# Moving the w_down stores to SyncE and three of eight outer products to VectorE in the feed-forward stage of a training-step kernel

## The chip, the cores and the metric

The kernel runs on one core of one Trainium2 chip. Its time is the device time of one execution in microseconds. The core has five instruction streams that run beside each other: TensorE (PE: matmuls and transposes), VectorE (DVE), ScalarE (ACT), GpSimd (POOL) and SyncE (SP). In this kernel POOL and SP do nothing but issue DMA transfers, except for a few constants that POOL builds at the start. Each of them takes its transfers strictly in the order of the program: one whose semaphores are not there yet holds up all that stand behind it. Three runs of the kernel before took 605.4, 604.7 and 602.12 us, so the median is 604.7 us.

## The reference

The reference is the forward and the backward pass of one decode step of a transformer block with one token (a row `x` of 1024 numbers). The six modulation vectors are `silu(c) @ w_mod`; then comes attention of 32 heads over the last 4096 rows of a key/value cache of 65536 rows, and then a feed-forward part:

```
g = x @ w_gate;  u = x @ w_up            # 1024 -> 3584
y = (sigmoid(g) * u) @ w_down            # 3584 -> 1024
```

The outputs are the result row and the gradients with respect to the input row, both caches, and all weight matrices. Two facts shape the work. The gradient of the caches is zero outside the 4096 rows, yet all of it must be written: about 126 MB of zeros. And the gradient of each weight matrix is an outer product of two vectors, so that each weight is read once and a matrix of the same size is written: there is little arithmetic for many bytes. For the feed-forward part, the gradients of `w_up` and `w_gate` are outer products of the normalised row `h2` with `dug` (the gradient at `u` and `g`), and that of `w_down` is one of the hidden vector with the gradient of the output.

## The kernel before

All large tiles lie in one on-chip array, `arena`; buffers are places in it, and the order of all instructions is written out by hand (`tc.manual_schedule()`), engine by engine. Dependences become semaphore waits. The 120 zero regions, 1 MB each, are stores that `zero(n)` (line 153) puts into POOL's stream at fixed places, `n` at a time from tables such as `Z_FFN`, as filling between the other transfers.

The stages follow each other: loads and attention (to about 155 us of the profile), a long matmul stage for the gradient of the output projection (`bch`, line 692, to about 285 us), the feed-forward stage (about 310 to 483 us), and a last stage that writes the gradients of the attention weights, of `w_mod` and of the caches (to the end at 605 us). The change touches the feed-forward stage alone.

That stage goes over seven blocks `q` of 512 hidden units. A block holds 2 MB of `w_up` and `w_gate` in `ug_v`, which has two buffers (`q % 2`), each in eight pieces `j` of 128 rows; and 1 MB of `w_down` in `wd_v`, which has one buffer in two halves `s` of 0.5 MB. Every buffer is used in place: the weights are loaded, read, overwritten with their own gradient, stored, and the weights of a later block are loaded over them.

In one pass of the loop (line 1017) these steps follow each other:

1. For each `j`: `ttr` (line 210, DVE) multiplies the piece of block `q` with the broadcast row `dug_b`, writes the product over the piece and sums it into `dh2acc`; then `outer_act` (line 241, ACT) overwrites the piece with `h2[j] * dug_b`. At `j` 0, 2, 5 and 6 a `side()` job is put in ahead of the outer product: eight PE transposes of another tensor into the one `mm` bank of PSUM (line 837), and an ACT copy of the result (line 838).
2. `store_ug` (line 869, POOL) stores pieces 0 to 3 after `j == 3` and pieces 4 to 7 after the loop, two transfers of 0.5 MB each time.
3. `front(q+1)` (line 954, PE) multiplies the next block's weights with `h2`, `gates` (lines 959 and 960, ACT) takes two sigmoids, `hh_ops` (line 193, DVE) forms the hidden vector.
4. For each half `s` of `w_down`: `ffn_mm` (line 971, PE), `wd_ttr` (two `ttr` on DVE, writing `junk`) and `wd_outer` (two `outer_dve`, line 206, DVE), and then `store_wd` (line 855), which POOL issues.
5. `dug_part` (lines 193, 990 and 991; DVE, PE, ACT) makes the next `dug_b`.
6. Loads for later blocks: `load_ug(q+2, 0, 4)` and `load_ug(q+2, 4, 4)` (line 865, POOL) into the buffers that block `q` leaves, and `load_wd(q+2, 0)`, `load_wd(q+2, 1)` (line 852, SP).

Three orders matter. In POOL's stream of one block stand, in this order: `load_ug` of pieces 0 to 3, `store_wd` of half 0, `store_wd` of half 1, `load_ug` of pieces 4 to 7, two zero regions, `store_ug` of pieces 0 to 3, one zero region, `store_ug` of pieces 4 to 7. A `load_ug` waits until the `store_ug` of the same pieces has landed. In SP's stream stand the `load_wd` alone, each of which waits until the `store_wd` of its half has landed. Transfers of POOL share eight completion semaphores in turn, and so do those of SP and ACT together.

In the last block there is no `side()`; instead ACT copies six parked tiles back from PSUM (`unpark`, line 1000), three of them within the loop over `j`, at 3, 5 and 6.

Of the kernel before, what the change touches and what calls it, by code (L numbers as in the profile page):

```python
# [58 lines left out]
def kernel(  # L59
# [26 lines left out]
    nc = tc.nc  # L86
# [13 lines left out]
    def ar(off, size):  # L100
        return arena[:, int(off * KIB):int((off + size) * KIB)]

    def vt(shape, name, dt=FP32):
        return pool.tile(shape, dt, name=name)
# [47 lines left out]
    def zero(n, after=None):  # L153
        for _ in range(n):
            if len(zleft) <= keep[0]:
                return
            region, narrow_ = zleft.pop(0)
            first = None
            if narrow_:
                nc.gpsimd.inc_swdge_sem([], [], mode="reset_dge_cursor")  # L160
                n = nlen - ncount.pop()
                first = nc.gpsimd.dma_start(
                    out=rest[0:NS, 0:nlen * 128].rearrange("p (t x) -> p t x", t=2)[:, :, n * 64:(n + 1) * 64],
                    in_=zeros[0:NS, 0:64].rearrange("p (t x) -> p t x", t=1).broadcast_to([NS, 2, 64]))
                ins = nc.gpsimd.dma_start(
                    out=region[8:P, :].bitcast(FP32).rearrange("(t p) x -> p t x", t=2),
                    in_=zeros[0:60, :].rearrange("p (t x) -> p t x", t=1).broadcast_to([60, 2, ZW // 2]))
            else:
                ins = nc.gpsimd.dma_start(out=region.bitcast(FP32), in_=zeros[:, :])  # L169
            if after is not None:  # L170
                dep(first or ins, after)
# [26 lines left out]
    def addv(out, a, b):  # L198
        return tt(out, a, b, ALU.add)

    def cp(out, a):
        return nc.vector.tensor_copy(out=out, in_=a)  # L202
# [6 lines left out]
    def ttr(out, w, b, acc):  # L209
        return nc.vector.tensor_tensor_reduce(out=out, in0=w, in1=b, scale=1.0, scalar=0.0,  # L210
                                              op0=ALU.mult, op1=ALU.add, accum_out=acc)
# [28 lines left out]
    def outer_act(out, col, b):  # L240
        return nc.scalar.activation(out=out, in_=b, func=ACT.Copy, scale=col)  # L241
# [203 lines left out]
    def side(n=1):  # L445
        for _ in range(n):
            if jobs:
                jobs.pop(0)()
# [177 lines left out]
    for g in range(G):  # L626
        nbank = bank_pair("n_ps", g)
        for t_ in range(KT):
            s = g * KT + t_
# [216 lines left out]
    wd_v = ar(152, 8).rearrange("p (i d) -> p i d", i=4)  # L846

    def wd_dram(t, q, s):
        return t[q * FB + s * 256:q * FB + s * 256 + 256, :].rearrange("(p j) d -> p j d", j=2)

    def load_wd(q, s):
        nc.sync.dma_start(out=wd_v[:, 2 * s:2 * s + 2, :], in_=wd_dram(B_w_down, q, s))

    def store_wd(q, s):
        nc.gpsimd.dma_start(out=wd_dram(out_8, q, s), in_=wd_v[:, 2 * s:2 * s + 2, :])

    def ug_part(view, q, j0, n):
        return view[:, j0:j0 + n, q * FB:(q + 1) * FB]
# [4 lines left out]
    def load_ug(q, j0, n):  # L863
        for k, view in ((0, wu_view), (1, wg_view)):
            nc.gpsimd.dma_start(out=ug_tile(q, k, j0, n), in_=ug_part(view, q, j0, n))

    def store_ug(q, j0, n):
        for k, view in ((0, dwu_view), (1, dwg_view)):
            nc.gpsimd.dma_start(out=ug_part(view, q, j0, n), in_=ug_tile(q, k, j0, n))  # L869
# [17 lines left out]
    h2 = vt([P, KD], "h2")  # L887
# [49 lines left out]
    dug_b = scr  # L937
# [10 lines left out]
    def front(q):  # L948
        gu = gu_t[q % 2]
        for col, k in ((4, 0), (0, 1)):  # L950
            for i in range(4):
                f0 = 256 * (i // 2) + i % 2
                for j in range(KD):
                    nc.tensor.matmul(gu[:, col + i:col + i + 1], lhsT=ug_v[:, q % 2, j // 4, j % 4, k, f0:f0 + 255:2],
                                     rhs=h2_bf[:, j:j + 1], start=(j == 0), stop=(j == KD - 1))

    def gates(q):
        r, gu = small[q % 2], gu_t[q % 2]
        nc.scalar.activation(out=r["sg"], in_=gu[:, 0:4], func=ACT.Sigmoid)
        nc.scalar.activation(out=r["om"], in_=gu[:, 0:4], func=ACT.Sigmoid, scale=-1.0)  # L960

    def hh_ops(q):
        r, up = small[q % 2], gu_t[q % 2][:, 4:8]
        mulv(r["hh_bf"], r["sg"], up)
        mulv(r["hh"], r["sg"], up)
        mulv(r["hom"], r["hh"], r["om"])

    def ffn_mm(q, s):
        for i in (2 * s, 2 * s + 1):
            for k in range(KD):  # L970
                nc.tensor.matmul(ffn_ps[:, k:k + 1], lhsT=wd_v[:, i, k * P:(k + 1) * P],  # L971
                                 rhs=small[q % 2]["hh_bf"][:, i:i + 1], start=(i == 0 and k == 0),
                                 stop=(i == 3), skip_group_check=True)

    def wd_ttr(q, s):
        for i in (2 * s, 2 * s + 1):
            ttr(junk, wd_v[:, i, :], b1k, small[q % 2]["dhh"][:, i:i + 1])

    def wd_outer(q, s):
        for i in (2 * s, 2 * s + 1):  # L980
            outer_dve(wd_v[:, i, :], small[q % 2]["hh"][:, i:i + 1], b1k)
        store_wd(q, s)

    def dug_part(q):
        r = small[q % 2]
        mulv(r["dug_bf"][:, 0:4], r["dhh"], r["sg"])
        mulv(r["dug_bf"][:, 4:8], r["dhh"], r["hom"])
        tp = new_tp("tp_dug")
        for i in range(8):
            nc.tensor.transpose(tp[:, i * P:(i + 1) * P], r["dug_bf"][:, i:i + 1].broadcast_to([P, P]), ident_bf[:, :])  # L990
        nc.scalar.copy(out=dug_b.rearrange("p (s f j) -> p s f j", s=4, j=2),  # L991
                       in_=tp.rearrange("p (s j f) -> p s f j", s=4, j=2))
# [6 lines left out]
    def unpark(p):  # L999
        nc.scalar.copy(out=B_home[p], in_=BT_ps[p][:, :])  # L1000
# [16 lines left out]
    for q in range(NB):  # L1017
        z = Z_FFN[q]
        more = q + 1 < NB
        for j in range(KD):  # L1020
            w = ug_v[:, q % 2, j // 4, j % 4, :, :].rearrange("p k f -> p (k f)")
            ttr(w, w, dug_b, dh2acc[:, q * KD + j:q * KD + j + 1])
            if more and j in (0, 2, 5, 6):
                side()
            if not more and j in (3, 5, 6):
                unpark({3: 2, 5: 0, 6: 4}[j])
            outer_act(w, h2[:, j:j + 1], dug_b)
            if j == 0:
                if q == 0:
                    cp(ffn, ffn_ps)  # L1030
                else:
                    addv(ffn, ffn, ffn_ps)
            if j == 3:
                store_ug(q, 0, 4)
                zero(z[0])
        store_ug(q, 4, 4)
        zero(z[1])
        if more:
            front(q + 1)
            gates(q + 1)  # L1040
            side()
            hh_ops(q + 1)
            ffn_mm(q + 1, 0)
            wd_ttr(q + 1, 0)
            if q + 2 < NB:
                load_ug(q + 2, 0, 4)
            wd_outer(q + 1, 0)
            zero(z[2])
            side()
            ffn_mm(q + 1, 1)  # L1050
            wd_ttr(q + 1, 1)
            side()
            dug_part(q + 1)
            wd_outer(q + 1, 1)
            if q + 2 < NB:
                load_ug(q + 2, 4, 4)
            zero(z[3])
            if q + 2 < NB:
                load_wd(q + 2, 0)
                load_wd(q + 2, 1)  # L1060
        else:
            zero(z[2] + z[3])
# [32 lines left out]
    for b in range(2):  # L1095
        for i in range(KD):
            for a in range(4):
                w = wo_t[4 * b + a].rearrange("p a (i d) -> p i a d", i=KD)
# [236 lines left out]
```

## Time and profile before

| | before |
|---|---|
| runs | 605.4, 604.7, 602.12 us; median 604.7 us |
| span of the profiled execution, first to last instruction | 605.5 us |
| busy, share of the span: PE / DVE / ACT / POOL | 68% / 54% / 47% / 29% |
| bytes moved, mean rate | 246.63 MB, 407 GB/s |
| of these by POOL's queue / by SP's queue | 233.33 MB / 12.59 MB |
| one `ttr` of a piece, DVE, 128x1024 bf16 | 1223 ns |
| one outer product of a piece on ACT (line 241, 56 of them) | 1146 ns |
| one outer product of the same shape on DVE (line 206, 28 of `w_down`) | 481 ns median |
| one `store_wd` from issue to landing, POOL, 0.5 MB | 3.9 / 8.2 / 13.6 us (least, median, most) |
| one `load_wd` from issue to landing, SP, 0.5 MB | 8.9 / 12.3 / 15.8 us |

No time of the profiled execution other than its span is given; the span lies 0.8 us above the median of the runs and 0.1 us above the slowest. The busy shares are means over stages with different limits. [...] The two rows at the bottom hold the time that a transfer stands in the queue behind others, so they tell more about the length of the queue than about the transfer.

### The profile page before, as it was taken

What the parts mean: (1) busy time and instruction counts of PE and PEld (TensorE: products, weight loads), DVE (VectorE), ACT (ScalarE), POOL (GpSimd) and SP (SyncE); (2) the same over time, 40 slices, a digit from 0 to 9 for tenths busy, and PEclk for the clock granted to TensorE, in tenths of its full rate; (3) what the DMA queues carried; (4) which work ended last, traced back from release to release, by engine and by line L of the source; (5) the groups of instructions that cost most, each with busy time, mean ns of one, the idle gap of its engine ahead of it and who ended that gap; (6) DMA issues with size and microseconds to landing.
All of it is one profiled execution on the core that took longest, in us unless ns stands there. A gap on an engine that the chain in (4) does not pass through costs nothing.

```text
span 605.5 us, 11074 instructions
## 1 busy us (share of the span) xinstructions
PE 413.7 (68%) x4612; PEld 277.5 (46%) x4612; DVE 327.2 (54%) x620; ACT 284.6 (47%) x429; POOL 174.6 (29%) x278
## 2 busy tenths in 40 slices
PE   3997789999999989899964345435444196865300
PEld 3995434334345446556653234334334175565300
DVE  3754499999411020150028286595686887768530
ACT  3489515557211024212227476765856845873200
POOL 3203113222223122222232233343433282122330
PEclk9999699999999999999975555555555566755555
DMA  8999999999999999999999999999999999999995
GB/s 350 419 417 423 414 426 417 428 424 425 427 420 425 425 425 421 427 423 423 419 402 409 407 328 387 389 377 412 389 390 416 422 422 412 421 424 427 423 415 245
DMA packets 45026, 246.63 MB, mean 407 GB/s; under 512 B 5085, under 2 KB 5085, under 8 KB 24544
## 3 DMA queue, kind: packets, MB, share of 16 engines
q0 software_dynamic: 41136, 233.33, 100.7%
q1 hardware_dynamic: 3792, 12.59, 5.7%
q8 instruction: 36, 0.59, 0.4%
q14 instruction: 14, 0.11, 0.0%
q10 hardware_dynamic: 48, 0.01, 0.0%
HBM read 60.30 MB, written 185.60 MB: 406 GB/s over the span
## 4 chain that ended last, share of the span: by engine, by line
DMA 41%; PE 29%; DVE 17%; issue 5%; ACT 5%; POOL 0%; ACTq 0%; POOLq 0%; SPq 0%; DVEq 0%
DMA out_dram<-arena 18%; PE b_ps L692 10%; DMA arena<-in_B_w_down_dram 10%; DMA out_dram<-zeros 9%; PE n_ps L637 6%; DVE junk L210 5%; DVE arena L193 4%; DVE arena L210 3%; DMA arena<-in_B_w_gate_dram 3%; DVE arena L206 2%; PE t_ps L599 2%; PE tp_wq L454 2%; PE w_ps L395 2%; PE tp_k L435 1%; ACT arena L456 1%
## 5 line engine op out<-in xcount | busy, mean ns | idle before, releaser
L692 PE MATMUL b_ps<-arena 128*128 128x512 bf16 x512 | 116.2, 379 | 0.0
L169 POOL DMA_DIRECT2D out_dram<-zeros x114 | 62.2, 548 | 170.8 <-DMA out_dram<-zeros 55.5
L837 PE MATMUL tp_side<-ident_bf,arena 128*128 128x128 bf16 x432 | 53.3, 306 | 45.2 <-ACT arena L838 38.3
L838 ACT COPY arena<-tp_side 128x1024 bf16<-128x1024 bf16 x54 | 53.9, 1012 | 59.9 <-PE tp_side L837 59.5
L193 DVE TENSOR_TENSOR arena<-arena 128x2048 bf16<-128x2048 bf16 x64 | 76.5, 1224 | 2.3 <-PE n_ps L637 0.3
L692 PEld LDWEIGHTS <-arena 128*128 128x128 bf16 x512 | 48.7, 98 | 55.8 <-issue 2.9
L210 DVE CUSTOM_DVE_ANT_0 arena<-arena,scr 128x1024 bf16<-128x1024 bf16 x56 | 65.2, 1223 | 10.0 <-ACT scr L991 10.0
L637 PE MATMUL n_ps<-arena 128*128 128x512 bf16 x256 | 65.7, 378 | 6.2 <-DVE arena L193 4.6
L837 PEld LDWEIGHTS <-arena 128*128 128x128 bf16 x432 | 44.3, 142 | 49.6 <-issue 49.3
L241 ACT ACTIVATE arena<-scr,h 128x1024 bf16<-128x1024 bf16 x56 | 61.5, 1146 | 1.4 <-DVE dh2acc L210 1.3
L637 PEld LDWEIGHTS <-arena 128*128 128x128 bf16 x256 | 24.6, 97 | 41.6 <-issue 16.2
L210 DVE CUSTOM_DVE_ANT_0 junk<-arena,b1k 128x1024 bf16<-128x1024 bf16 x28 | 34.3, 1223 | 15.4 <-DMA arena<-in_B_w_down_dram 14.8
L1162 ACT ACTIVATE arena<-ps_kv 128x512 bf16<-128x512 f32 x48 | 26.2, 686 | 26.3 <-PE ps_kv L1158 26.2
L869 POOL DMA_DIRECT2D out_dram<-arena x28 | 21.3, 765 | 57.2 <-ACT arena L241 32.6
L202 DVE CAST arena<-b_ps 128x512 bf16<-128x512 f32 x6 | 4.2, 692 | 61.6 <-PE b_ps L692 61.6
L601 ACT CAST arena<-t_ps 128x512 bf16<-128x512 f32 x56 | 30.1, 589 | 12.1 <-PE t_ps L599 12.1
L1158 PE MATMUL ps_kv<-junk,arena 8*128 8x128 bf16 x256 | 27.4, 306 | 10.5 <-DVE arena L206 9.5
L1158 PEld LDWEIGHTS <-arena 8*128 8x128 bf16 x256 | 25.4, 142 | 12.3 <-issue 12.3
L971 PE MATMUL fg<-hh_bf,arena 128*128 128x1 bf16 x224 | 8.2, 166 | 29.9 <-DMA arena<-in_B_w_down_dram 29.2
L456 ACT COPY arena<-tp_wq 128x1024 bf16<-128x1024 bf16 x23 | 21.7, 1044 | 8.2 <-PE tp_wq L454 8.2
L971 PEld LDWEIGHTS <-arena 128*128 128x128 bf16 x224 | 7.2, 105 | 33.1 <-DMA arena<-in_B_w_down_dram 32.4
L878 ACT CAST arena<-fold_ps 128x512 bf16<-128x512 f32 x16 | 9.4, 586 | 24.1 <-PE fold_ps L876 24.1
(302 smaller groups left out, 662.8 us busy)
## 6 DMA issues: line engine op xcount, KB each, us to landing
out_dram<-zeros POOLq DMA_DIRECT2D x114, 1024.0 KB, 15.3
out_dram<-arena POOLq DMA_DIRECT2D x32, 1024.0 KB, 18.2
out_dram<-arena POOLq DMA_DIRECT2D x50, 512.0 KB, 11.1
arena<-in_A_wq_dram POOLq DMA_DIRECT2D x8, 1024.0 KB, 20.5
arena<-in_A_wo_dram POOLq DMA_DIRECT2D x8, 1024.0 KB, 12.8
arena<-in_w_mod_dram POOLq DMA_DIRECT2D x7, 1024.0 KB, 18.5
arena<-in_B_w_down_dram SPq DMA_DIRECT2D x14, 512.0 KB, 12.3
arena<-in_B_w_up_dram POOLq DMA_DIRECT2D x14, 512.0 KB, 8.0
```

Of the source, the lines that this page charges most:

```text
L169: ins = nc.gpsimd.dma_start(out=region.bitcast(FP32), in_=zeros[:, :])
L193: return nc.vector.tensor_tensor(out=out, in0=a, in1=b, op=op)
L210: return nc.vector.tensor_tensor_reduce(out=out, in0=w, in1=b, scale=1.0, scalar=0.0, op0=ALU.mult, op1=ALU.add, accum_out=acc)
L241: return nc.scalar.activation(out=out, in_=b, func=ACT.Copy, scale=col)
L456: nc.scalar.copy(out=blk, in_=tp[:, :])
L601: nc.scalar.copy(out=o, in_=ps)
L637: mm = nc.tensor.matmul(nbank[k][:, :], lhsT=k_nat[:, g, t_ * DH:(t_ + 1) * DH], rhs=vp[:, t_ % 2, 4 * k:4 * k + 4, :].rearrange("p h d -> ...
L692: mm = nc.tensor.matmul(bbank[p][k][:, :], lhsT=a4[:, p, h, :], rhs=wo_t[u][:, a, k * 512:(k + 1) * 512], start=(i == 0 and a == 0), stop= ...
L837: nc.tensor.transpose(tp[:, i * P:(i + 1) * P], blk[:, i * P:(i + 1) * P], ident_bf[:, :])
L838: nc.scalar.copy(out=blk if dst is None else dst, in_=tp[:, :])
L1158: nc.tensor.matmul(ps[:, t4 * DH:(t4 + 1) * DH], lhsT=rows[32 * g:32 * g + HG, t_ * P:(t_ + 1) * P], rhs=hd[32 * g:32 * g + HG, :], start= ...
L1162: nc.scalar.activation(out=o, in_=ps[:, :], func=ACT.Copy, scale=float(scale))
```

## The change

Three edits are made at once.

First, `store_wd` is issued by SP instead of POOL: 14 stores of 0.5 MB leave POOL's stream and join the `load_wd` in SP's. SP's stream is then, for each block, two stores and two loads. POOL's stream of a block loses two transfers between `load_ug` of pieces 0 to 3 and `load_ug` of pieces 4 to 7.

Second, of the eight outer products of a block the last three (`j` 5, 6 and 7) go from ACT to DVE, each just after the `ttr` of its piece: 21 over the seven blocks.

Third, the four `side()` jobs of a block stand after the outer products of `j` 1, 2, 3 and 4 and no longer ahead of those of `j` 0, 2, 5 and 6. PE's order stays the same, instruction by instruction. In the last block the `unpark` copies stay where they were, so that ACT now makes five of the six after its last outer product.

```diff
     def store_wd(q, s):
-        nc.gpsimd.dma_start(out=wd_dram(out_8, q, s), in_=wd_v[:, 2 * s:2 * s + 2, :])
+        nc.sync.dma_start(out=wd_dram(out_8, q, s), in_=wd_v[:, 2 * s:2 * s + 2, :])
...
         for j in range(KD):
             w = ug_v[:, q % 2, j // 4, j % 4, :, :].rearrange("p k f -> p (k f)")
             ttr(w, w, dug_b, dh2acc[:, q * KD + j:q * KD + j + 1])
-            if more and j in (0, 2, 5, 6):
-                side()
             if not more and j in (3, 5, 6):
                 unpark({3: 2, 5: 0, 6: 4}[j])
-            outer_act(w, h2[:, j:j + 1], dug_b)
+            (outer_act if j < 5 else outer_dve)(w, h2[:, j:j + 1], dug_b)
+            if more and 0 < j < 5:
+                side()
             if j == 0:
```

## The prediction

> **What bounds the kernel now.** I read the page first, then the feed-forward stage in windows, then POOL's and DVE's timelines there, and the table of waits last. The page's second part:
>
> ```profile
> DVE  3754499999411020150028286595686887768530
> ACT  3489515557211024212227476765856845873200
> DMA  8999999999999999999999999999999999999995
> GB/s 350 419 417 423 414 426 417 428 424 425 427 420 425 425 425 421 427 423 423 419 402 409 407 328 387 389 377 412 389 390 416 422 422 412 421 424 427 423 415 245
> ```
>
> No compute engine is full for long; the 16 DMA engines are busy in every slice, and most slices move 415 to 428 GB/s. So bytes bound the kernel: 246.63 MB at about 420 GB/s is 587 us. Time can be won only where the rate drops, and it drops in slices 23 to 29, the feed-forward stage. The windows of that stage (the columns are busy time and instruction count of each engine, then clock, DMA share, GB/s):
>
> ```profile
> 348.00:360.00 12.00, 5.53 (x56) 4.62 (x57) 9.96 (x20) 7.43 (x8) 3.75 (x6) 0.50 0.88 306
> ...
> 372.00:396.00 24.00, 10.20 (x158) 8.94 (x159) 15.99 (x33) 16.12 (x18) 8.72 (x13) 0.50 1.04 381
> 396.00:420.00 24.00, 11.24 (x165) 9.45 (x163) 16.99 (x37) 16.22 (x18) 9.00 (x14) 0.50 1.05 392
> 420.00:444.00 24.00, 10.72 (x160) 9.20 (x160) 16.22 (x33) 16.54 (x19) 9.97 (x15) 0.50 1.06 396
> 444.00:468.00 24.00, 10.56 (x160) 9.12 (x160) 17.31 (x37) 16.73 (x19) 10.12 (x16) 0.50 1.06 400
> 468.00:492.00 24.00, 10.70 (x152) 6.49 (x153) 19.49 (x56) 16.58 (x18) 10.02 (x14) 0.57 1.11 419
> ```
>
> Against 418 GB/s, the first window (a hole) loses 12 x (1 - 306/418) = 3.2 us; the four block periods of 24 us, at 392 on average, lose 96 x (1 - 392/418) = 6.0 us. These 9.2 us are all there is to win. After 468 us the rate is full.
>
> The hole's cause is in POOL's timeline:
>
> ```profile
> 344.80 0.75 POOL L865 DMA_DIRECT2D arena<-in_B_w_up_dram  x1 [5.70 <-issue]
> 345.93 0.76 POOL L865 DMA_DIRECT2D arena<-in_B_w_gate_dram  x1 [0.37 <-PE tp_side L837]
> 348.04 0.56 POOL L855 DMA_DIRECT2D out_dram<-arena  x1 [1.36 <-DVE arena L206]
> 352.46 0.56 POOL L855 DMA_DIRECT2D out_dram<-arena  x1 [3.87 <-DVE arena L206]
> 353.01 0.77 POOL L865 DMA_DIRECT2D arena<-in_B_w_up_dram  x1
> ```
>
> POOL waits 3.87 us for DVE's `w_down` product and holds the second pair of `load_ug` behind it. The stores that this pair needs had landed at 349.9 and 351.2 us by the trace, the loads went out at 353.0 and 353.8, and the engines ran dry between. In the later blocks the same order costs otherwise: at 419.99 POOL issues a `load_ug` when the store before it has landed, and only at 422.11 the `store_wd` whose product DVE had ended at about 418.7. The waits:
>
> ```profile
> DVE hh_bf L193 <- ACT om L960: 27.5, 7, 4.1
> ...
> POOL out_dram L855 <- DVE arena L206: 16.9, 7, 3.9
> ...
> DVE junk L210 <- DMA arena<-in_B_w_down_dram: 14.8, 6, 6.6
> ...
> SPq L852 <- DMA out_dram<-arena: 139.6, 12, 30.6
> ```
>
> DVE waits 4.1 us a block for ACT's sigmoids, which stand behind ACT's last outer products, and 2.3 us a block for `w_down`. That makes a loop: store 7.6 us to landing (398.2 to 405.9), load 9.5 (to 415.4), DVE 3.3, POOL's delay 3.4; sum 23.8 against the 23.7 us from block to block (from DVE's first `w_down` sum at 392.05 to 415.44 and 439.77, 23.9 on average).
>
> **What the skill says.** The Trainium skill, DMA: Bandwidth & Descriptors, section Issuing engines are not separate DMA queues: transfers from all issuers run on the same 16 DMA engines and interleave, and another issuer saves sequencer time alone. The trace agrees: with an SP load in flight, 435 to 437 us moves 424 GB/s in all, no more than without. So SP brings no bandwidth, only another order. The same page, section SWDGE vs HWDGE vs iDMA: POOL's descriptors are written by GpSimd, which a VectorE operation in a two-port mode locks out; SP's are immune. Here the trace shows five POOL issues taking 7.05 us (1.41 each) at 490.7 us beside DVE's scalar products, against 0.55 to 0.77 elsewhere.
>
> **The change, part by part.**
>
> *ACT to DVE.* In each block ACT loses 3 x 1.15 = 3.4 us. DVE gains three products, 481 ns alone and 0.44 in succession (0.88 a pair, timeline): 3 x 0.44 = 1.3 us. Take the block whose first `ttr` starts at 423.57. DVE ends at 423.57 + 8 x 1.145 + 1.3 = 434.0 (before 432.9). ACT's chain becomes two products, copy, product, copy, product, copy, product, copy: from 424.7, 5 x 1.1 + 4 x 1.0 = 9.5, to about 434.3 (before 436.75). The last `store_ug` can go at 434.3, not 437.1: 2.8 us earlier. The sigmoids gain less, since PE's fourth transpose still waits for ACT's third copy (432.3), then transposes 1.0 and runs `front`, 1.8: sigmoids at about 435.5, 1.3 us earlier. On the path that sets the end: nothing in blocks where the DMA queue is never empty, for DVE's work hides under 23.7 us of transfers. POOL issues meanwhile may be locked out for 3 x 0.48 = 1.4 us a block; their landing is 7 to 14 us after issue, which hides it; without that cover 1.4 x 7 = 10 us.
>
> *The last block* has 1.3 us more of DVE work ahead of the reduction at 480.30 that opens the last stage. The cover is the queue: a zero region issued at 488.9 landed at 502.6, 13.7 us later. Cost 0; without cover +1.3.
>
> *Stores to SP.* POOL loses 14 x 0.58 = 8.1 us of issue time and 16.9 us of waiting. SP gains 14 issues; its own is 0.33 us (`load_wd`), so 4.6 us on a stream that waits nearly always. SP's new order puts `load_wd` of half 0 behind `store_wd` of half 1, which waits for DVE 3.3 us longer; but that load waits 7.6 us for its own store anyway: cost 0, while landing stays above 3.3. In the hole the loads go out at landing + 0.6, as at 395.63 to 396.22: 350.5 and 351.8 instead of 353.0 and 353.8, 2.0 to 2.5 us earlier. With the two stores running on the other queue meanwhile, I take 2.7 of the hole's 3.2 us; bounds 0 (the dry spot moves to a later load) and 3.2.
>
> In the four later periods the queue is never empty, so the earlier `store_wd` (3.4 us) and the ended waits for `w_down` and ACT move nothing by themselves. What remains is the short queue when `load_ug` goes out: it lands 7 to 8 us after issue there, and the 2 us windows from 423, 425 and 429 us move only 340, 363 and 328 GB/s. The earlier `w_down` traffic lies ahead of those loads and fills part of this. I take 0.45 us of the 1.5 lost in each: 4 x 0.45 = 1.8. Bounds: 1.5 each, or less than nothing, since taking 1 MB out of POOL's queue shortens it (the 2.5 us that 1 MB takes at 418 GB/s lies on the other queue): -1.5 each.
>
> Sum: -2.7 - 1.8 + 0 = -4.5 us; 605.5 becomes 601.0. The span stands 0.8 above the median of the runs, so I forecast 604.7 - 4.5 = 600.2 us. The last stage passes the gain on: its queue is 8 us or more deep, and DVE waits there for its stores (13.6 us in all).
>
> **Rivals.**
>
> *All of it:* both losses go, -9.2 us: 595.5. For: compute gains slack in every block. Against: a `load_ug` still follows the landing of its own store, so the short queue stays.
>
> *Nothing to be seen:* bytes bound the blocks and the hole stays, because `load_wd` (6.6 us of DVE's wait ahead of it) lands no earlier: the zero regions that POOL no longer holds behind `store_wd` go first. Gain 0 to 2.5: about 603.5.
>
> *Slower:* the SP queue is served late. What SP issues today lands after 12.3 us (median), POOL's `store_wd` after 8.2. The loop would be store X + load 9.5 + DVE 3.3 with POOL's delay gone: it passes 23.7 from X = 10.9 us. At X = 12.3 it is 25.1, 1.4 us more in each of five periods, and the hole grows instead of closing: 7 + 1 = 8, so 612.7. For it: both transfers of the loop then stand in the slower queue, and a deeper POOL queue lengthens both. Against: steady loads landed in 8.9 to 9.5 us, and a loop that runs late drains the queue that delays it.
>
> **How the numbers follow.** A difference of about 0.5% (3 us: 601.7 to 607.7) is what a measurement here can tell from none; the three runs themselves spread by that. Chances: forecast (a gain of 3 to 7) 0.42, all of it 0.13, nothing 0.27, slower 0.18. Faster is 0.55, same 0.27, slower 0.18. Cases of both signs are in it: the forecast's own range is 597.5 to 601.7. The range of 8 in 10 goes from 595.5, the full gain, to 609, which takes in all but the worse two thirds of the slow case.
>
> **What would show it.** Right: a rate near 390 where 306 stood, no POOL wait for DVE at line 855, `load_ug` issued 0.6 us after its store's landing, DVE's 4.1 us for the sigmoids down to about 1.5, ACT 24 us less busy (21 x 1.15) and DVE 10 more, the same bytes, and block periods of 23.0 to 23.5 us. Wrong: `store_wd` from SP landing after more than 10.9 us, with DVE's wait for `w_down` grown; POOL issues of over 0.9 us in the blocks; or windows under 390 GB/s after 396 us, the shorter POOL queue running dry.

## The result and the profile after

The changed kernel takes 601.16 us (median of 7 runs, 600.37 to 602.82) against 603.67 us for the kernel before (median of 7, 602.12 to 611.53): ratio 0.9963, 95% interval [0.9945, 0.9981]. In a second comparison it was 601.89 us (14 runs) against 603.38 (43 runs), ratio 0.9979 [0.9961, 0.9998]. So the change wins 0.2 to 0.4%, 1.3 to 2.2 us by the ratios. The forecast was a gain of 4.5 us, 0.74%: right in sign, two to three and a half times too large, and as a time (600.2 us) 1.0 to 1.7 us too low.

The profiled execution of the changed kernel has a span of 598.5 us and took 600.56 us in all. Its span is 7.0 us below the 605.5 us of the profile shown of before, and the medians differ by only 2.5. The two profiles are single executions, and that of before stood near the upper end of its runs. A good part of this document is about telling the kernel from the execution.

The page's second part, of the changed kernel (40 slices of the span; the lines of VectorE, ScalarE, the DMA engines and the bytes moved):

```profile
DVE  3653499999511010160007598795796887768530
ACT  2489514567212014213225565673664746873200
DMA  8999999999999999999999999999999999999996
GB/s 348 420 417 421 414 427 413 427 423 425 428 419 425 423 427 424 422 424 423 423 397 412 420 387 413 406 398 414 406 404 412 420 422 412 421 424 426 424 416 279
```

Slices 24 to 30 (counted from 1; the prediction counts them from 0), where 328 and then 377 to 412 stood, now hold 387 and then 398 to 414. The rest is as it was. The windows of the feed-forward stage, changed kernel (busy time and count of TensorE's matmuls, its weight loads, VectorE, ScalarE, POOL; then clock, DMA share, GB/s):

```profile
348.00:360.00 12.00, 5.09 (x52) 4.44 (x51) 10.82 (x20) 9.48 (x10) 4.91 (x8) 0.50 1.13 394
...
372.00:396.00 24.00, 10.80 (x161) 9.48 (x160) 18.66 (x41) 14.33 (x16) 7.70 (x11) 0.50 1.10 408
396.00:420.00 24.00, 10.80 (x160) 9.54 (x160) 17.43 (x38) 13.13 (x16) 8.04 (x12) 0.50 1.10 405
420.00:444.00 24.00, 10.63 (x160) 9.47 (x160) 19.24 (x40) 14.96 (x17) 8.99 (x13) 0.50 1.09 407
444.00:468.00 24.00, 9.79 (x152) 8.60 (x151) 18.41 (x38) 14.33 (x16) 7.84 (x13) 0.50 1.12 411
```

The hole rose from 306 to 394 GB/s and the four periods from 381, 392, 396 and 400 to 405 to 411. Against 418 GB/s the loss in the hole went from 3.2 us to 12 x (1 - 394/418) = 0.7, and in the periods from 6.0 to 96 x (1 - 408/418) = 2.3: 6.2 of the 9.2 us, in this pair of executions.

POOL's timeline at the hole, changed kernel (start, duration, engine, line, operation, tiles; in brackets the idle time before it and what ended it):

```profile
344.63 0.88 POOL L865 DMA_DIRECT2D arena<-in_B_w_up_dram  x1 [7.13 <-DMA out_dram<-arena]
347.55 0.75 POOL L865 DMA_DIRECT2D arena<-in_B_w_gate_dram  x1 [2.05 <-issue]
349.91 0.75 POOL L865 DMA_DIRECT2D arena<-in_B_w_up_dram  x1 [1.60 <-DMA out_dram<-arena]
351.47 0.75 POOL L865 DMA_DIRECT2D arena<-in_B_w_gate_dram  x1 [0.82 <-PE tp_side L837]
352.21 1.13 POOL L169 DMA_DIRECT2D out_dram<-zeros  x2
```

No `store_wd` stands in the stream any more, and the second `load_ug` pair goes out at 349.9 and 351.5 us, 3.1 and 2.3 us earlier than in the profile shown of before. The waits of the whole execution, changed kernel (us in total, times, longest):

```profile
POOL arena L865 <- DMA out_dram<-arena: 35.0, 11, 7.2
DVE hh_bf L193 <- ACT om L960: 20.6, 7, 5.2
ACT sg L959 <- PE fg L954: 20.4, 7, 4.9
PEld L954 <- DMA arena<-in_B_w_gate_dram: 10.7, 5, 2.5
DVE junk L210 <- DMA arena<-in_B_w_down_dram: 5.7, 2, 5.1
```

POOL's 16.9 us of waiting for VectorE are gone, and VectorE's waits for `w_down` fell from 14.8 to 5.7 us. What has grown is the wait of POOL's `load_ug` for a store to land: 35.0 us in 11 waits, where the table of before has this line:

```profile
POOL arena L865 <- DMA out_dram<-arena: 9.6, 6, 5.0
```

The traces put many of these waits down to another releaser, so the whole is the safer figure: all idle time of POOL just before a `load_ug` rose from 44.0 to 69.2 us, while the 17.3 us before a `store_wd` went. VectorE's wait for the sigmoids stayed at 20.6 us of 27.5. ScalarE, its chain now shorter, waits for `front`, and `front` in five of the seven blocks for `load_ug`. The new wait stands in the same loop, one link further on.

### The profile page after: what moved, and what is told of

Same layout as the page of the kernel before. It is cut to its first block, busy times and chain, and to the rows that moved or that the text cites. A ratio compares the mean times of both kernels' runs of the same rounds, so it can differ in the third digit from the quotient of the medians.

```text
span 598.5 us, 11039 instructions
## 1 busy us (share of the span) xinstructions
PE 408.8 (68%) x4587; PEld 275.9 (46%) x4612; DVE 336.6 (56%) x641; ACT 266.2 (44%) x408; POOL 166.8 (28%) x264
## 4 chain that ended last, share of the span: by engine, by line
PE 43%; DMA 26%; DVE 17%; ACT 6%; issue 5%; POOL 0%; ACTq 0%; POOLq 0%; SPq 0%; DVEq 0%
PE b_ps L692 17%; DMA out_dram<-arena 15%; DMA arena<-in_B_w_gate_dram 7%; PE n_ps L637 6%; DVE arena L206 4%; DVE arena L193 4%; DVE arena L210 3%; DVE junk L210 3%; PE t_ps L599 2%; DMA arena<-in_B_w_down_dram 2%; PE tp_side L837 2%; ACT arena L838 2%; PE tp_wq L454 2%; PE w_ps L395 2%; PE tp_k L435 1%
## 5 line engine op out<-in xcount | busy, mean ns | idle before, releaser
L692 PE MATMUL b_ps<-arena 128*128 128x512 bf16 x494 | 113.4, 379 | 1.0 <-issue 0.2
L837 PE MATMUL tp_side<-ident_bf,arena 128*128 128x128 bf16 x432 | 51.7, 300 | 48.8 <-ACT arena L838 41.9
L692 PEld LDWEIGHTS <-arena 128*128 128x128 bf16 x512 | 48.7, 98 | 55.9 <-issue 2.9
L837 PEld LDWEIGHTS <-arena 128*128 128x128 bf16 x432 | 43.4, 139 | 53.8 <-issue 53.4
L241 ACT ACTIVATE arena<-scr,h 128x1024 bf16<-128x1024 bf16 x35 | 40.1, 1148 | 9.6 <-DVE dh2acc L210 7.8
L637 PEld LDWEIGHTS <-arena 128*128 128x128 bf16 x256 | 24.6, 97 | 41.6 <-issue 16.2
L1162 ACT ACTIVATE arena<-ps_kv 128x512 bf16<-128x512 f32 x48 | 26.1, 681 | 27.9 <-PE ps_kv L1158 27.5
L865 POOL DMA_DIRECT2D arena<-in_B_w_up_dram x14 | 10.7, 762 | 51.6 <-DMA out_dram<-arena 29.1
L954 PE MATMUL fg<-h_bf,arena 128*128 128x1 bf16 x448 | 14.7, 166 | 12.5 <-DMA arena<-in_B_w_gate_dram 10.3
L206 DVE TENSOR_SCALAR arena<-arena,cs_col 128x4096 bf16<-128x4096 bf16 (+1 forms) x16 | 16.0, 1018 | 7.5 <-DMA out_dram<-arena 7.5
## 6 DMA issues: line engine op xcount, KB each, us to landing
arena<-in_A_wq_dram POOLq DMA_DIRECT2D x8, 1024.0 KB, 20.6
```

The lines of the kernel that those rows point to most:

```text
L206: return nc.vector.tensor_scalar(out=out, in0=a, scalar1=s1, scalar2=None, op0=op0)
L637: mm = nc.tensor.matmul(nbank[k][:, :], lhsT=k_nat[:, g, t_ * DH:(t_ + 1) * DH], rhs=vp[:, t_ % 2, 4 * k:4 * k + 4, :].rearrange("p h d -> ...
L692: mm = nc.tensor.matmul(bbank[p][k][:, :], lhsT=a4[:, p, h, :], rhs=wo_t[u][:, a, k * 512:(k + 1) * 512], start=(i == 0 and a == 0), stop= ...
L837: nc.tensor.transpose(tp[:, i * P:(i + 1) * P], blk[:, i * P:(i + 1) * P], ident_bf[:, :])
L1162: nc.scalar.activation(out=o, in_=ps[:, :], func=ACT.Copy, scale=float(scale))
```

## Experiments

Theories as the runs were planned. A: POOL's stream, which held `load_ug` behind a store that waits for VectorE, is what cost, so SyncE's stores alone bring the gain. B: the work taken off ScalarE brings it. C: both are needed. D: the sizes in the profile of before belong to its one execution. E, formed after the second group: what counts is how many bytes are outstanding when POOL, after waiting for a store to land, issues `load_ug`. F, against E: a second queue, or POOL relieved of the stores, is what helps.

**The parts of the change, each by itself.** The stores alone:

```diff
     def store_wd(q, s):
-        nc.gpsimd.dma_start(out=wd_dram(out_8, q, s), in_=wd_v[:, 2 * s:2 * s + 2, :])
+        nc.sync.dma_start(out=wd_dram(out_8, q, s), in_=wd_v[:, 2 * s:2 * s + 2, :])
```

> Only the w_down stores move to SyncE; the outer products stay on ScalarE. Theory A (the gain comes from POOL's in-order stream, which held the second pair of load_ug behind the store that waits for VectorE): the window 348 to 360 us goes from 306 to at least 385 GB/s, POOL's wait of 16.9 us at line 855 is gone, and nearly the whole gain is here: 2 to 3 us, ratio 0.995 to 0.9967. Theory B (the gain comes from the work taken off ScalarE, which issues the second store_ug 2.8 us earlier): no more than 0.5 us, ratio 0.999 to 1.001, the later block periods still 23.7 us. Theory C (both are needed): 1 to 1.5 us here, the hole closed and the later periods unchanged.

Measured: 601.73 us against 603.16, ratio 0.9981 [0.9958, 1.0005]. Twelve of its 14 runs lie between 600.69 and 602.38, two above 606, and the profiled one is one of these two (606.25). POOL's wait for VectorE is gone and the hole stands at 391 GB/s, as theory A expected; but 1.1 to 1.4 us is the size that theory C expected of this run, less than A's 2 to 3.

The three products alone:

```diff
-            outer_act(w, h2[:, j:j + 1], dug_b)
+            (outer_act if j < 5 else outer_dve)(w, h2[:, j:j + 1], dug_b)
```

> Only the three outer products of each block move from ScalarE to VectorE; ScalarE's copies keep their places in the block's order and the w_down stores stay with POOL. Theory A: VectorE's 1.3 us a block and ScalarE's 3.4 us a block both hide under the transfers: ratio 0.999 to 1.001, the hole still at about 306 GB/s. Theory B: 1.5 to 2.5 us faster, ratio 0.996 to 0.9975, block periods of 22.6 to 23.2 us. A third outcome, POOL's issues locked out beside VectorE's products: up to 1.4 us a block, ratio up to 1.01, issues at lines 865 and 869 of over 0.9 us in the blocks.

Measured: 603.86 us (14 runs), ratio 1.0008 [0.9988, 1.0027].

The products and the places of ScalarE's copies, that is, everything but the stores:

```diff
-            if more and j in (0, 2, 5, 6):
-                side()
...
-            outer_act(w, h2[:, j:j + 1], dug_b)
+            (outer_act if j < 5 else outer_dve)(w, h2[:, j:j + 1], dug_b)
+            if more and 0 < j < 5:
+                side()
```

> Everything of the change but the queue of the w_down stores, which POOL still issues: three outer products on VectorE, ScalarE's copies behind its outer products. Theory A: nothing, ratio 0.999 to 1.001, because POOL still holds the second pair of load_ug behind the store (hole at 300 to 330 GB/s). Theory B: the whole gain, ratio 0.995 to 0.9975. Theory C (both are needed): 0.5 to 1 us, the later periods at about 23.2 us and the hole open. With the run before it the difference is what the places of the copies are worth: 0 by every theory but B.

Measured: 602.71 us (22 runs), ratio 0.9996 [0.9985, 1.0008].

The first comparison puts the gain with the stores, without yet separating the stores' interval from 1; theory B is out. POOL's issues were not held up beside VectorE's products either: the mean `store_ug` issue (line 869) is 768 ns in both runs, 765 in the profile of before, and no issue at lines 865 and 869 took more than 842 ns.

**The order in POOL's stream, without SyncE.** The second `load_ug` pair moves ahead of the second `w_down` store, which stays on POOL:

```diff
-            wd_outer(q + 1, 1)
             if q + 2 < NB:
                 load_ug(q + 2, 4, 4)
+            wd_outer(q + 1, 1)
```

> The stores stay with POOL and ScalarE keeps its outer products; only the order in POOL's stream changes: the second pair of load_ug is issued ahead of the second w_down store of its block, not behind it. Theory A in its narrow form (it is the order alone that costs): the second pair goes out at about 350.5 and 351.8 us instead of 353.0 and 353.8, the hole rises to at least 370 GB/s, and the gain is that of SyncE's stores alone: 1.5 to 3 us, ratio 0.995 to 0.9975. If a second queue is what helps (the w_down traffic gets a place of its own in the 16 engines), this run gains under 0.5 us, while SyncE's stores alone gain 2 or more. If the w_down store, now waiting for load_ug's slot, becomes late itself: VectorE's wait for w_down grows from 2.3 us a block, and the run is no faster or slower, up to 1.005.

Measured: 603.52 us (22 runs), ratio 1.0009 [0.9997, 1.0021], no gain. Its windows:

```profile
348.00:360.00 12.00, 4.07 (x32) 3.42 (x33) 10.65 (x22) 8.27 (x9) 3.84 (x7) 0.50 1.03 364
...
372.00:396.00 24.00, 10.59 (x161) 9.12 (x160) 16.80 (x35) 16.34 (x19) 9.18 (x14) 0.50 1.04 380
```

The loads went out early (350.0 and 351.5 us) and the hole is 364 (at least 370 was expected), the other three periods stand at 404 to 407, and VectorE's wait for `w_down` fell to 5.2 us; yet the time did not move. The narrow form of theory A, that the hold-up in POOL's order costs the time, falls.

**Both kernels once more, and the stores alone beside them.** No edit in the first two.

> The kernel before, unchanged, profiled a second time. It asks how much of the profile shown of before is the kernel and how much the one execution, which at 605.5 us of span stood 1 us or more above the median of its runs. Theory D (the lags of before in the feed-forward stage change from execution to execution): this profile shows a hole and later periods of other sizes, the byte lag gained between 142 and 190 MB is 4 to 8 us and not 10.1, and the ratio is 1.000 within 0.001. If the sizes belong to the kernel: again 10 us of lag, 306 GB/s in the hole and 381 to 400 after it.

Measured: 604.06 us (14 runs) against 603.38, ratio 1.0007 [0.9990, 1.0023]: the kernel before against itself gives 1 within its interval. Its second profile (span 602.7, run time 604.54, close to its median) shows another hole. Windows, then POOL's timeline, of this second execution of before:

```profile
348.00:360.00 12.00, 4.29 (x35) 3.65 (x36) 10.57 (x23) 9.30 (x10) 5.49 (x9) 0.50 1.03 379
...
372.00:396.00 24.00, 11.34 (x168) 9.90 (x169) 17.18 (x37) 16.23 (x18) 9.02 (x13) 0.50 1.06 396
396.00:420.00 24.00, 10.76 (x163) 9.23 (x161) 16.61 (x35) 16.23 (x18) 8.94 (x13) 0.50 1.07 402
420.00:444.00 24.00, 10.41 (x160) 8.97 (x159) 16.21 (x34) 16.34 (x18) 9.60 (x15) 0.50 1.05 388
444.00:468.00 24.00, 10.22 (x158) 8.69 (x157) 15.87 (x34) 16.23 (x18) 8.67 (x14) 0.50 1.06 395
```

```profile
347.82 0.56 POOL L855 DMA_DIRECT2D out_dram<-arena  x1
349.57 0.56 POOL L855 DMA_DIRECT2D out_dram<-arena  x1 [1.20 <-DVE arena L206]
350.31 0.77 POOL L865 DMA_DIRECT2D arena<-in_B_w_up_dram  x1 [0.18 <-issue]
351.68 0.78 POOL L865 DMA_DIRECT2D arena<-in_B_w_gate_dram  x1 [0.60 <-PE tp_side L837]
```

The hole is 379 and not 306, the store waits 1.20 us and not 3.87, and the loads go out at 350.3 and 351.7 us, within 0.2 us of the times that the prediction gave to the changed kernel. The hole of 306 was that execution's, as theory D had it. The later periods are alike in these two executions, 388 to 402 here and 381 to 400 there; that they can differ as well is seen further down.

> The changed kernel, unchanged, beside the others of this group on one chip. By its first comparison: ratio 0.9945 to 0.998, 600.4 to 602.8 us. Its profile shows again a lag of 3.5 to 5 us gained between 142 and 190 MB if the changed kernel runs evenly (theory D: the change takes away the executions with large lags rather than a fixed amount from each).

Measured: 601.89 us, ratio 0.9979 [0.9961, 0.9998]; profile with a span of 599.7 and 601.79 us in all, again close to its median. Its four periods stand at 406, 406, 408 and 406 GB/s, as in the first profile of this kernel, and its hole at 383, hardly above the 379 of the second profile of before.

> The w_down stores alone on SyncE, a second time and beside the whole change on one chip. Theory A: within 0.5 us of the whole change. Theory C (both parts are needed): 1 us or more behind it, the later periods at 24 us in the profile, with the hole closed.

Measured: 601.48 us (22 runs), ratio 0.9970 [0.9958, 0.9983]. The stores alone are as fast as the whole change on the same chip (601.89). With the first comparison of it this settles where the gain sits, against B and C: it is the stores', and the products and the copies add nothing that can be measured. It does not yet say how the stores bring it, for A's reason fell with the change of POOL's order.

**Where the bytes fall behind.** From the records of all DMA packets I worked out, for each profile, when the n-th megabyte had moved, and how far that lies behind n at 420 GB/s. The stretch from 142 to 150 MB is the hole, 150 to 190 MB the four periods after it. Beside it stand the bytes outstanding (of transfers issued by any engine, not yet moved) at the moment of each of 16 `load_ug` issues after the hole: their mean, and the mean of the shallower of a block's two pairs. (The recorded expectations further down give this quantity 0.53 MB lower, because they count the packets that fetch instructions, about 0.5 MB up to there, as moved bytes of these transfers.)

| profile | outstanding, MB | in the shallower pair | lag 142-150, us | lag 150-190, us | lag 190-246, us |
|---|---|---|---|---|---|
| before, as shown | 1.40 | 1.27 | 3.8 | 6.3 | -0.1 |
| before, second | 1.47 | 1.38 | 1.6 | 5.7 | 0.0 |
| POOL's order changed | 1.56 | 1.28 | 1.9 | 4.7 | -0.1 |
| stores on SyncE, first (606.25 us) | 1.61 | 1.31 | 1.1 | 6.2 | 0.0 |
| stores on SyncE, second | 1.82 | 1.42 | 1.0 | 4.0 | 0.0 |
| all but the stores | 1.62 | 1.58 | 1.8 | 3.3 | 0.0 |
| products alone | 1.82 | 1.82 | 1.1 | 2.6 | -0.1 |
| whole change, as shown | 1.90 | 1.54 | 1.2 | 2.9 | 0.0 |
| whole change, second | 1.92 | 1.54 | 1.3 | 3.1 | 0.0 |

What these profiles lose between 142 and 190 MB is never given back or added to later. On the whole, with more outstanding, less is lost. The mean doesn't tell all: at 1.6 MB one profile loses 6.2 us and another 3.3, and there the shallower pair (1.31 and 1.58) tells them apart. Nor are the later periods the same in each execution of a kernel: the stores on SyncE alone lose 6.2 us in one and 4.0 in the other. For the two kernels' second profiles, which stand near their medians, the sum over the stage is 7.3 and 4.4 us: 2.9 of the 3.0 us between their spans. (The profiles of "products alone" and "all but the stores" are from the lower ends of their runs, 600.85 us where the median is 603.86, and 601.47 where it is 602.71, so their lags are not typical of those kernels.)

How the stores deepen the queue is seen in the traces around the `load_ug` of 415 to 420 us. The profile shown of before, POOL:

```profile
414.75 1.50 POOL L869 DMA_DIRECT2D out_dram<-arena  x2 [5.06 <-ACT arena L838]
419.99 0.75 POOL L865 DMA_DIRECT2D arena<-in_B_w_up_dram  x1 [3.75 <-PE tp_side L837]
421.28 0.84 POOL L865 DMA_DIRECT2D arena<-in_B_w_gate_dram  x1 [0.53 <-DMA out_dram<-arena]
422.11 1.10 POOL L855 DMA_DIRECT2D out_dram<-arena  x2
```

The changed kernel, SP and POOL:

```profile
413.80 4.03 SPq L855 DMA_DIRECT2D out_dram<-arena  x2
```

```profile
414.81 0.75 POOL L865 DMA_DIRECT2D arena<-in_B_w_up_dram  x1 [7.17 <-DMA out_dram<-arena]
416.09 0.75 POOL L865 DMA_DIRECT2D arena<-in_B_w_gate_dram  x1 [0.53 <-issue]
```

In before POOL issues a `store_ug` pair at 414.75 and then waits until 419.99, just after the store that its `load_ug` needs has landed (419.39); the `w_down` stores come behind that pair of loads, though VectorE had ended the first product at 418.7. In the changed kernel SyncE sends the first of them at 413.80, during POOL's wait and ahead of the `load_ug` at 414.81. At the first pair of each later block 2.25 MB is outstanding, against 1.27; at the second pair it is the same, 1.54 in both. POOL's changed order fits this too: first pair 1.83, second 1.28, the deficit moved and not filled.

**The dose, up and down.** If that is the cause, bytes that depend on nothing, put ahead of `load_ug`, do the same. Each block has three zero regions of 1 MB, which wait for nothing in the stage; `Z_FFN` says how many go out behind the first `store_ug` pair, behind the second, after the first and after the second `load_ug` pair. With the whole change:

```diff
-Z_FFN = [(1, 0, 0, 2)] * 5 + [(1, 1, 1, 2), (1, 2, 1, 0)]
+Z_FFN = [(1, 1, 0, 1)] * 5 + [(1, 1, 1, 2), (1, 2, 1, 0)]
```

> The whole change, and in five blocks one of the two zero regions that POOL issues behind the second load_ug pair goes out behind the second store_ug pair instead, ahead of the first load_ug; the bytes are the same. It tests the last step of the prediction, that what is left in the periods is the short queue when load_ug goes out. If so, a deeper queue fills the dips: 0.3 to 0.6 us in each of five blocks, 1.5 to 3 us faster than the whole change, about 598 to 599.5 us. If the loop of store, load and VectorE binds instead: load_ug lands about 1.2 us later, each of five periods grows by up to that, and the run is 1 to 6 us slower than the whole change, VectorE and TensorE waiting longer for load_ug.

Measured: 599.38 us (6 runs), ratio 0.9940 [0.9921, 0.9959], faster than the whole change by 2.5 us. Windows:

```profile
348.00:360.00 12.00, 4.96 (x44) 4.22 (x42) 10.81 (x20) 9.57 (x10) 4.34 (x7) 0.50 1.08 411
...
372.00:396.00 24.00, 10.99 (x163) 9.73 (x163) 17.96 (x38) 14.60 (x16) 7.88 (x11) 0.50 1.09 413
396.00:420.00 24.00, 10.66 (x160) 9.36 (x159) 17.55 (x37) 13.08 (x15) 8.15 (x12) 0.50 1.09 409
```

Outstanding 2.32 MB, lags 0.3 and 2.2 us, and 0.5 us more after 190 MB. The decisive run is the same line in the kernel before, with its stores on POOL:

> The kernel before, with its stores on POOL and its products on ScalarE; only the zero regions of five blocks move: one of the two behind the second load_ug pair goes out ahead of the first. Theory E (a block loses what the queues run dry of while POOL, whose load_ug waits for a store to land, issues nothing; the bytes outstanding at that moment decide): the 0.6 to 1.1 MB outstanding at the first load_ug pair become 1.5 MB or more, the lag from 142 to 190 MB falls from 7.3 to 10 us to 4 us or less, and the run is at least as much faster as SyncE's stores make it: 1.5 to 4 us, ratio 0.9935 to 0.9975. Rival F (it takes the second queue, or POOL relieved of the stores): no gain, ratio 0.999 to 1.003, because each load_ug lands up to 2.5 us later in a loop that runs through POOL.

Measured: 599.89 us (22 runs), ratio 0.9943 [0.9926, 0.9959], by its ratio faster than the change under study, without any of its edits. Windows:

```profile
324.00:336.00 12.00, 7.19 (x133) 6.55 (x132) 7.65 (x18) 4.33 (x7) 1.62 (x4) 0.50 0.53 193
...
372.00:396.00 24.00, 11.90 (x183) 10.56 (x184) 17.76 (x39) 16.99 (x19) 10.88 (x16) 0.50 1.07 410
396.00:420.00 24.00, 11.05 (x164) 9.26 (x161) 17.22 (x37) 16.84 (x19) 8.79 (x14) 0.50 1.07 412
420.00:444.00 24.00, 11.76 (x181) 10.18 (x182) 17.88 (x39) 16.84 (x19) 9.69 (x15) 0.50 1.07 412
444.00:468.00 24.00, 11.29 (x166) 9.50 (x163) 16.98 (x35) 16.34 (x19) 9.11 (x14) 0.50 1.07 413
```

Outstanding 2.65 MB, lags 0.9 and 2.0. All four periods are at 410 or more with POOL issuing the stores, so theory F falls. (This profile is of the one run of 22 that took 606.69 us, the others 599.04 to 600.85: it lost 7.2 us at 324 to 336 us, before the blocks begin, where VectorE's first product came late. The blocks themselves are what is read here.) The runs also lie closer together: 21 of the 22 within 1.8 us, where the 52 runs of before beside them spread over 6.6 us, 600.82 to 607.38.

The same line with the stores on SyncE and no products moved:

> The w_down stores on SyncE and the zero regions moved, ScalarE keeping all its outer products. Theory A with E: as fast as the whole change with the zero regions moved, 599 to 600 us, ratio 0.9925 to 0.9955, since the products' engine has moved nothing so far. If VectorE's three products are what lets the later load_ug be borne (ScalarE then ends 2.8 us later in each block): 1 us or more slower than that, 600.5 to 602 us.

Measured: 599.42 us (7 runs), ratio 0.9938 [0.9915, 0.9961]; outstanding 2.81 MB, lags 0.8 and 2.1. With the zero region moved, the three kernels (none of the change, the stores, all of it) have ratios of 0.9943, 0.9938 and 0.9940: once the queue is deep, neither the stores' queue nor the products' engine is worth anything that these runs can tell.

The opposite dose on the whole change, all three regions at the block's end:

```diff
-Z_FFN = [(1, 0, 0, 2)] * 5 + [(1, 1, 1, 2), (1, 2, 1, 0)]
+Z_FFN = [(0, 0, 0, 3)] * 5 + [(1, 1, 1, 2), (1, 2, 1, 0)]
```

> The whole change, and the zero region between the two store_ug pairs of five blocks goes to the end of the block as well, so that all three stand behind the second load_ug pair: the opposite dose. Theory E: what is outstanding at the first load_ug falls from 1.5 to 1.9 MB to under 1 MB, each of five blocks loses 0.5 us or more against the whole change, 603 to 607 us, most of what the stores on SyncE had brought or more. Rival F: no change from the whole change, or up to 1 us faster since load_ug lands sooner: 600.5 to 602 us.

Measured: 603.70 us (14 runs), ratio 1.0000 [0.9982, 1.0017]: the whole gain is gone with the change still in. Outstanding at the first pairs 1.33 MB, 1.46 over all, lags 2.9 and 5.4, as in the kernel before. A window and a wait of this run:

```profile
372.00:396.00 24.00, 11.83 (x168) 10.23 (x168) 20.01 (x41) 14.68 (x16) 7.71 (x11) 0.50 1.09 389
```

```profile
POOL arena L865 <- DMA out_dram<-arena: 51.0, 13, 9.9
```

Too much of it:

```diff
-Z_FFN = [(1, 0, 0, 2)] * 5 + [(1, 1, 1, 2), (1, 2, 1, 0)]
+Z_FFN = [(1, 2, 0, 0)] * 5 + [(1, 1, 1, 2), (1, 2, 1, 0)]
```

> The whole change, with both late zero regions of five blocks behind the second store_ug pair. Theory E alone: no dip at load_ug is left at all, a further 0 to 1 us under the run with one region moved, 598.4 to 599.4 us. If the loop binds from here: load_ug lands up to 2.5 us later than with one region moved, VectorE's and TensorE's waits for it grow past what they can catch up, and the run is 1 to 8 us slower than that one; the second load_ug pair then finds an emptier queue behind it.

Measured: 604.32 us (22 runs), ratio 1.0008 [0.9996, 1.0020]. Outstanding 3.69 MB and the hole at 411 GB/s, but the lag from 150 to 190 MB is 5.2 us, and 2.5 us more is lost after it. POOL's timeline of this run:

```profile
374.24 0.79 POOL L865 DMA_DIRECT2D arena<-in_B_w_gate_dram  x1 [0.54 <-issue]
384.47 1.53 POOL L869 DMA_DIRECT2D out_dram<-arena  x2 [9.44 <-ACT arena L241]
```

Behind the second `load_ug` pair POOL now has nothing until ScalarE's products, which wait for the late loads: 9.44 us. From 384 to 387 us the engines move 296 GB/s. The dry spot has moved to the other end of the block. The loop binds, as the second expectation had it.

## Why the prediction was right or wrong

**What bounds the kernel: right.** Bytes bound it, and what differs between the profiles is lost in the feed-forward stage. In the table no kernel loses anything after 190 MB.

**"The hole's cause", 2.7 us of the sum: the step that failed.** It took a wait of 3.87 us, seen once, for a property of the kernel. In the second execution of before the wait is 1.20 us, the hole costs 1.6 us of lag and not 3.8, and the changed kernel's hole costs 1.2 to 1.3. So the term is about 0.3 us in the two executions that stand near their medians. The run that removed the hold-up inside POOL's stream gained nothing. Nothing in the profile shown said how typical the hole was; the three runs, with a spread of 3.3 us, did say that executions differ by as much as the term.

**"The four later periods", 1.8 us: the mechanism was right, the size was not.** The step named the short queue when `load_ug` goes out, and `w_down` traffic ahead of it as what fills it, at 0.45 us a period. The lag over these periods fell from 5.7 to 3.1 us in the second profiles, 2.6 us, 0.65 a period; the blocks came at 22.9 us on average (from VectorE's first `w_down` sum of the second block to that of the last: 114.5/5 in the profile shown, 114.6/5 in the second) instead of 23.7 and 23.9. A block carries 9 MiB, 9.44 MB; at 420 GB/s that is 22.5 us, so little is left. The forecast of 23.0 to 23.5 us was a shade too long. The 2.6 us rest on one profile of each kernel, and two profiles of one kernel differed by 2.2 us of such lag; the medians, 1.5 to 2.5 us apart, bear out no more than the order of size. The prediction's lower bound, that the shorter POOL queue costs as much, did not come: what went with the loss was the sum over both queues. That fits the Trainium skill, DMA: Bandwidth & Descriptors, section Issuing engines are not separate DMA queues, by which the transfers of all issuers run on the same 16 DMA engines and interleave; and with one zero region moved the time was the same with the stores on POOL and on SyncE, 599.89 and 599.42 us.

**The loop's sum** of store, load, VectorE and POOL's delay, 23.8 us, fitted the period, but does not set it. POOL's delay of 3.4 us was taken out and the period fell by 0.8 to 1.0 us. Bytes and dry spots set the period. The loop sets it only when the loads are made late, as in the last run.

**ACT to DVE, nothing: right**, by 0.9996 [0.9985, 1.0008] and 1.0008 [0.9988, 1.0027]. The engine times were near: ScalarE's busy time fell by 18.4 us where 24 was forecast (its outer products from 61.5 to 40.1), and VectorE gained 9.4 where 10 was. A lock-out of POOL's issues did not show where the products moved and the stores stayed; in the changed kernel two issues of the blocks took 0.97 and 0.99 us, just over the 0.9 that the prediction named as a bad sign, 0.2 us each above the rest. The 1.41 us that it took for each issue at 490.7 us is a mean of unequal ones: the first took 3.51 us, until VectorE's row of products had ended, the four others 0.77 to 0.95. The sigmoid wait, forecast at 1.5 us a block, is 20.6/7 = 2.9 in the changed kernel (27.5/7 = 3.9 before) and now ends with `load_ug`, not with ScalarE's chain. With the stores left on POOL the moved products did shorten it, to 8.8 and 8.4 us in all, 1.2 a block, and the median did not move, so that wait did not set the time.

**Stores to SP, no cost: right as far as the span goes.** `store_wd` from SyncE lands after 8.8 us (median of the 4 of 14 landings that the trace gives), below the 10.9 us at which the rival "Slower" was to decide and far from its 12.3.

**The base.** The gain was summed against an execution of 605.5 us of span; the kernel before has medians of 603.2 to 604.1 us in five sets of 175 runs in all, against 604.7 in the three shown. In absolute time this error and the gain two to three and a half times too large partly cancelled, and 600.2 came out near 601.2 and 601.9. That the time fell into the forecast's own range (597.5 to 601.7) in the first comparison is in part luck: 2.7 of the 4.5 us of gain stood for a hole that the change closes by about 0.3 us, and in the second comparison it lies just outside.

**Of the rivals**, "Nothing to be seen" was the closest to the gain: 0 to 2.5 us. Its reason was half right: little of the hole was the change's to close. But `load_wd` did come earlier, for VectorE's wait for it fell from 14.8 to 5.7 us, and that bytes bound the blocks already was wrong by the 2.6 us. "All of it" needs a deeper queue at every `load_ug`; even the best runs keep 2.5 to 3 us of lag over the two stretches.

What stays open: the kernels with the products moved but POOL's stores show a deep queue and small lags in their one profile each, and no gain in their medians. Both profiles are of executions faster than the median, so they fit a queue that is deep in some executions and not in others; no second profile of these kernels shows which is the rule. Nor is it settled why some executions, with the stores on either queue, start the blocks 6 or 12 us late and lose 1.5 to 7.2 us between 134 and 142 MB. In the traces of all five a matmul of line 344, ahead of the blocks, sits 4.3 to 7.0 us idle, against 0.3 to 2.1 in the others, until a load of `w_mod` lands. Why that load comes late is not shown; this part of the program lies ahead of every edit here.

## What to carry to other kernels

When an in-order issuer waits for a landing and then starts the next load, look at the bytes outstanding over all queues at that moment, and fill it with traffic that depends on nothing; here one constant did more than two engines' rebalancing and a change of queue. Add it in steps, since each megabyte ahead of the load also delays it (by about 2.6 us here): one region moved brought 0.6%, two brought nothing. And size a term from a stall only after seeing the stall in a second execution, or after asking what in the runs' spread it could be.

## What the runs showed of the hardware

How deep the queue must be, over all issuers and at the moment when `load_ug` goes out, is told by the runs: with 1.4 to 1.5 MB on average the four periods lost 5.4 to 6.3 us, with 1.6 to 1.8 MB anything from 2.6 to 6.2, with 1.9 MB 2.9 to 3.1, with 2.3 to 2.8 MB 2.0 to 2.2, and with 3.7 MB 5.2 again, because the load itself came late.

Over the last 20 `load_ug` issues of each of fourteen profiles (280, 0.5 MB each) the time from issue to landing is, by a straight fit, 4.0 us plus 2.56 us for each MB outstanding, with a scatter of 1.0 us. So each megabyte ahead adds about the time that it takes to move, 2.4 us at 420 GB/s. Of the 4.0, the transfer's own 0.52 MB takes 1.2 us at 420 GB/s; by this estimate 2.8 us are left for what doesn't depend on the queue. It is a loose one, for within single profiles the slope lies between 0.3 and 2.6. The Trainium skill, DMA: Bandwidth & Descriptors, section Anatomy of one DMA — SWDGE (gpsimd) path, gives a fit of about 2.0 us plus the bytes at 436 GB/s for one DMA; here, behind other transfers, the constant comes out somewhat larger, and the measurement decides. The constant alone does not explain the depth that is needed: 2.8 us at 420 GB/s are 1.2 MB, and the kernel before had more than that outstanding when it lost most.

The time around the span differs between the kernels. With the `w_down` stores on POOL it is 1.78 to 1.84 us on average over the runs (604.54 - 602.7 in the second profile of before); with them on SyncE it is 2.10 to 2.12 us (600.56 - 598.5 in the profile of after) in five kernels, and 1.80 us in the sixth, the one with all three zero regions at the block's end. So in most of them 0.3 us of what SyncE's stores win inside the span is given back outside it. What it is made of no profile here shows.
